# Token mixing, an MLP and a normalized MLP on one core: normalization moved to ScalarE, weight conversions begun earlier, one ring for inner features

## The chip, the cores and the metric

The kernel runs on one core of one Trainium2 chip. The metric is the device time of one execution in microseconds; three runs of the kernel before are given, and one further execution was profiled. The engines are named as the profile does: PE (TensorE, with PEld for its weight loads), DVE (VectorE), ACT (ScalarE), POOL (GpSimd) and SP (SyncE, whose queue issues nearly all DMAs).

## The reference

Attention over 4 batches, 8 heads, 576 positions and 64 columns a head, causal in a window of 128 with a slope per head; then a block that mixes tokens and channels; then a normalized MLP. Cut to what matters:

```python
attn = softmax(where(mask, scale * q @ k.T + bias, -1e9)) @ v     # B, H, S, D = 4, 8, 576, 64
x = attn.transpose(0, 2, 1, 3).reshape(B, S, H * D)               # 512 columns
h = relu(x.transpose(0, 2, 1) @ w_tok1) @ w_tok2                  # 576 -> 256 -> 576
u = x + h.transpose(0, 2, 1)
x = u + relu(u @ w_ch1) @ w_ch2                                   # 512 -> 1536 -> 512
xn = (x - mean) / sqrt(var + 1e-6) * g_ln
out = x + relu(xn @ w2_ch1) @ w2_ch2                              # 512 -> 2048 -> 512
```

The weights come as 64-bit floats and everything is held in float32.

## The kernel before

**The work.** The 4 x 576 rows are 18 tiles of 128 rows; `u` holds them in SBUF from attention to the end. A float32 product is made of three matmuls on rounded parts: each operand is split into hi (a rounded copy, mostly on ACT) and lo (the operand minus hi, on DVE or POOL), and `mm3` adds hi x hi, hi x lo and lo x hi. A float64 weight tile is converted by `load_f64`: two DMAs (`rh`, `rw`), one instruction on ACT (`e`, L414) and four on DVE (`s` twice, L417 and L419; `m`, L421; the result `y` or `w`, L429).

**Stages.** `attention()` walks the tiles, and between the softmaxes of a tile it puts one conversion and some token mixing (`tok1`, `tok1_end`, `tok2`). Then come two MLP layers. Each goes over three chunks of tiles: 0 to 7, then 16 and 17, then 8 to 15; and in a chunk over steps of two tiles of inner features. The wide chunks multiply by Strassen's scheme with seven products (`seven_products`, L987 to L989), whose left operands `prep_wide` makes from turned quadrants of `u` (`turned`: transposes on PE, L841); the narrow chunk uses `prep_small` and `two_blocks` (L438 to L440). `relu_to` splits the inner features (L918 on ACT, L920 on DVE), and `second` (L1042 to L1044) multiplies them by the second weights and adds to `u` (DVE, L1047). In the second layer `turned` first normalizes each 128x128 block (L833, on DVE): minus mean, times rstd. Both come from `tile_stats` and `chunk_stats`, which run while another chunk is multiplied.

**Weights.** `load_w` fills a ring of 6 tiles `w` with weights in the order of use; it loads a staged copy from DRAM where there is one (`w<-d`) and converts otherwise. `stage_w` converts ahead and stores (`d<-y`). In attention, at slot n (two a tile), this decides:

```python
if W_START <= n < 2 * NTILE and (n - W_START) % W_STEP == 0:
    if len(wtiles) < W_BUFS:
        load_w(len(wtiles) + 1)
    else:
        stage_w(1)
```

With `W_START` 18 and `W_STEP` 2 this is 9 slots: 6 fill the ring, 3 stage.

**What sets the order.** Nothing runs in the order of the code: `op` only records an operation with a cost per engine that may run it, and `Plan.order` then plays a list schedule: each operation has a due time that follows from the place of PE's work behind it, engines take the most urgent one that is ready, and an operation with several engines goes where it ends first. What comes out is a fixed order for each engine's queue; each engine works through its queue strictly in that order, with semaphores between them. A change in one operation's cost or place thus moves others on all queues.

**Memory.** Pools are opened and closed by `swap`. A tile of a new pool can be written only when what lay in its place is no longer used. In the kernel before, the parts of split weights (`w1`, `w2`), the inner features `h` and the small operands `s` lie in pool `mlq`, which is opened when `tok` (token weights and features), `psb` and `pst` are closed in one step: behind the last use of all of them.

## Time and profile before

| what | value |
|---|---|
| median of 3 runs | 865.22 us |
| the runs | 863.85 to 865.59 us |
| the profiled execution | 863.28 us |
| its span, first to last instruction | 861.6 us |
| granted TensorE clock, mean | 0.992 |
| busy: PE, DVE, ACT, POOL | 834.8, 654.0, 367.7, 347.6 us |
| DMA bytes moved | 163.92 MB, 190 GB/s mean |

The granted clock is the share of TensorE's full 2.4 GHz that the throttle gave. A busy share is a mean over stages with different limits; which engine ends a wait is read in the stage. In a timeline the start of an instruction counts from the start of the span, and the bracket behind it says how long the engine had stood still before and which engine and line released it. Matmuls overlap, so their pace is the distance of their starts.

### The profile page before, as it was taken

The page shows a single profiled execution, that of the slowest core. Times are in us where ns is not written, and L with a number is a line of the kernel's source. Part 1 is how long each engine was busy: PE and PEld are TensorE (multiplying, and loading weights), DVE is VectorE, ACT ScalarE, POOL GpSimd, SP SyncE. Part 2 cuts the span into 40 slices and gives each one's busy share as a digit, 9 for nine tenths or more (in the row PEclk, how much of TensorE's full clock was granted, in tenths as well). Part 3 has the DMA queues.
Part 4 walks back from the last instruction along what each step waited for, and adds up shares of the span by engine and source line. Part 5 has one row for each costly group of instructions (what it writes and reads, how often), then busy time and mean ns, then how long its engine had stood idle before and what let it go on. Part 6 is the DMA issues. An engine that isn't in the chain of part 4 may idle for free.

```text
span 861.6 us, 13160 instructions
## 1 busy us (share of the span) xinstructions
PE 834.8 (97%) x4478; PEld 688.6 (80%) x4478; DVE 654.0 (76%) x1371; ACT 367.7 (43%) x880; POOL 347.6 (40%) x362
## 2 busy tenths in 40 slices
PE   7999999898999999999997999999999999999997
PEld 6777888676888888788886888888888888888886
DVE  5787676979888889978899956879779755555554
ACT  6888765553344535233355322333354322222221
POOL 2685444555343656522245434534145712221110
PEclk9999999989999999999999999999999999999999
DMA  8588534375778799977861521897377762221112
GB/s 294 184 226 259 186 114 148 110 239 157 246 223 275 265 328 319 355 248 250 279 211 37 194 85 64 257 300 233 126 257 216 242 215 74 74 73 49 49 50 97
DMA packets 73123, 163.92 MB, mean 190 GB/s; under 512 B 8289, under 2 KB 8417, under 8 KB 73057
## 3 DMA queue, kind: packets, MB, share of 16 engines
q1 hardware_dynamic: 72576, 161.78, 56.9%
q0 software_dynamic: 480, 1.31, 0.7%
q8 instruction: 35, 0.57, 0.3%
q14 instruction: 32, 0.25, 0.1%
HBM read 130.55 MB, written 31.20 MB: 188 GB/s over the span
## 4 chain that ended last, share of the span: by engine, by line
PE 65%; DVE 8%; DMA 1%; issue 1%; ACT 0%; SPq 0%; DVEq 0%; ACTq 0%
PE acc L1044 12%; PE acc L1042 12%; PE acc L1043 12%; PE b L987 9%; PE b L989 9%; PE b L988 9%; DVE st L833 2%; DVE u L1047 1%; DVE st L372 1%; PE b L438 1%; PE b L440 1%; PE p L841 1%; PE b L439 1%; DVE hl L920 1%; DVE xl L372 1%
## 5 line engine op out<-in xcount | busy, mean ns | idle before, releaser
L1047 DVE TENSOR_TENSOR u<-acc,u 128x512 f32<-128x512 f32 x252 | 172.3, 686 | 63.5 <-PE acc L1044 60.3
L1042 PE MATMUL acc<-w2h,hh 128*128 128x512 f32 x504 | 198.6, 394 | 2.0 <-DVE u L1047 1.3
L1044 PE MATMUL acc<-w2h,hl 128*128 128x512 f32 x504 | 197.1, 391 | 2.7 <-DVE hl L920 2.6
L1043 PE MATMUL acc<-w2l,hh 128*128 128x512 f32 x504 | 196.9, 391 | 0.0
L918 ACT ACTIVATE hh<-b 128x512 fp32r<-128x512 f32 (+1 forms) x140 | 74.5, 553 | 275.3 <-PE b L989 242.2
L989 PE MATMUL b<-xh,w1l 128*128 128x512 f32 x392 | 154.0, 393 | 2.8 <-DVE w1l L372 2.8
L987 PE MATMUL b<-xh,w1h 128*128 128x512 f32 x392 | 154.3, 394 | 2.2 <-DVE hl L920 1.2
L988 PE MATMUL b<-xl,w1h 128*128 128x512 f32 x392 | 153.5, 392 | 0.0
L920 DVE SCALAR_TENSOR_TENSOR hl<-b,hh 128x512 fp32r<-128x512 f32 (+1 forms) x140 | 85.4, 630 | 59.3 <-ACT hh L918 59.1
L372 POOL TENSOR_TENSOR w1l<-w,w1h 128x512 fp32r<-128x512 f32 (+1 forms) x53 | 68.3, 1289 | 148.9 <-ACT w1h L359 148.6
L1044 PEld LDWEIGHTS acc<-w2h,hl 128*128 128x128 f32 x504 | 94.9, 188 | 23.9 <-DVE hl L920 4.0
L1042 PEld LDWEIGHTS acc<-w2h,hh 128*128 128x128 f32 x504 | 95.2, 189 | 22.9 <-DVE u L1047 3.1
L1043 PEld LDWEIGHTS acc<-w2l,hh 128*128 128x128 f32 x504 | 95.1, 189 | 18.6
L372 POOL TENSOR_TENSOR w1l<-st,w1h 128x512 fp32r<-128x512 f32 x37 | 49.8, 1346 | 113.4 <-ACT w1h L359 102.9
L987 PEld LDWEIGHTS b<-xh,w1h 128*128 128x128 f32 x392 | 74.3, 190 | 18.8 <-DVE hl L920 2.0
L989 PEld LDWEIGHTS b<-xh,w1l 128*128 128x128 f32 x392 | 74.3, 189 | 18.8 <-DVE w1l L372 3.3
L988 PEld LDWEIGHTS b<-xl,w1h 128*128 128x128 f32 x392 | 74.2, 189 | 15.3
L414 ACT ACTIVATE e<-rh 128x512 bf16<-128x512 bf16 (+2 forms) x65 | 41.3, 636 | 65.9 <-DMA rh<-wb 39.8
L641 ACT ACTIVATE pr<-t,mn 128x128 f32<-128x128 f32 x144 | 55.9, 392 | 18.5 <-DVE mn L632 18.5
L658 POOL TENSOR_SCALAR_AFFINE_SELECT pf<-pf 128x512 f32<-128x512 f32 x64 | 42.2, 659 | 34.0 <-ACT pf L359 31.5
L372 DVE TENSOR_TENSOR b<-b,p 128x512 f32<-128x512 f32 x56 | 38.9, 695 | 19.5 <-PE b L989 19.2
L372 POOL TENSOR_TENSOR w2l<-w,w2h 128x512 fp32r<-128x512 f32 x23 | 31.1, 1357 | 47.1 <-ACT w2h L359 46.9
(117 smaller groups left out, 1373.0 us busy)
## 6 DMA issues: line engine op xcount, KB each, us to landing
w<-d SPq DMA_DIRECT2D x85, 256.0 KB, 4.1
rw<-wb SPq DMA_DIRECT2D x32, 512.0 KB, 5.0
rh<-wb SPq DMA_DIRECT2D x32, 512.0 KB, 4.4
rw<-wa SPq DMA_DIRECT2D x24, 512.0 KB, 4.2
rh<-wa SPq DMA_DIRECT2D x24, 512.0 KB, 4.6
d<-y SPq DMA_DIRECT2D x29, 256.0 KB, 4.5
keys<-kT SPq DMA_DIRECT2D x18, 256.0 KB, 4.1
q<-qT SPq DMA_DIRECT2D x18, 256.0 KB, 4.5
```

What stands on the lines that cost most here:

```text
L372: pl.op({e: cost[e] for e in on}, lambda e: ENGINE[e].tensor_tensor(get(), ga(), gb(), alu), [*several(a), *several(b), *also], several(dst))
L641: op({"ACT": 580}, lambda m=m: nc.scalar.activation(out=pr.t[:, m], in_=t.t[:, m], func=AF.Exp, bias=mn.t[:, m:m + 1], scale=-1.0, accum_o ...
L658: op({"POOL": 630}, lambda a=a: nc.gpsimd.affine_select(pf.t[:, a], pf.t[:, 1], [[0, 4], [1 - 2 * a, P]], (ALU.is_ge, ALU.is_gt)[a], 0.0, ...
L918: op({"ACT": act(n, True)}, lambda: nc.scalar.activation(out=hh.t[:, c], in_=go(), func=AF.Relu), [o], [(hh, key)])
L920: mark[0] = op({"DVE": dve(n)}, lambda: nc.vector.scalar_tensor_tensor(out=hl.t[:, c], in0=go(), scalar=0.0, in1=hh.t[:, c].bitcast(F32), ...
L987: nc.tensor.matmul(g.t, wh.t[:, w], xh.t, start=start and k == 0, stop=False, skip_group_check=True)
L988: nc.tensor.matmul(g.t, wh.t[:, w], xl.t, start=False, stop=False, skip_group_check=True)
L989: nc.tensor.matmul(g.t, wl.t[:, w], xh.t, start=False, stop=stop and k == 1, skip_group_check=True)
L1042: nc.tensor.matmul(o.t, hh.t[:, c:c + P], wh.t, start=j == 0, stop=False)
L1043: nc.tensor.matmul(o.t, hh.t[:, c:c + P], wl.t, start=False, stop=False)
L1044: nc.tensor.matmul(o.t, hl.t[:, c:c + P], wh.t, start=False, stop=j == 1)
L1047: op({"DVE": dve(DM)}, lambda o=o, i=i: nc.vector.tensor_tensor(u[i].t, o.t, u[i].t, ALU.add), [o], [u[i]])
```

## The change

Four things are changed, and the planner's order follows from them.

- **Normalizing.** L833's subtract and multiply on DVE becomes one activation on ACT: Identity with `rstd` as scale and a new column `nmr` as bias. `chunk_stats` gets one more instruction on DVE, which makes `nmr` = -mean x rstd.
- **Conversions in attention.** `W_START` goes from 18 to 12: 12 slots instead of 9, 6 of them to fill the ring, 6 to stage.
- **One ring.** The token features of `tok1_end` and the inner features of the MLPs take their tiles from one ring of 6 in a new pool `hid`, which is open from start to end. The token weights `wt2h`, `wt2l` and the small operands share one pair of tiles there (`few`).
- **Pools.** `tok` is closed by itself and `mlq`, which now holds only split weights, is opened in its place; `psb` and `pst` are closed in a step of their own. `load_w(W_BUFS)` is recorded ahead of `prep_wide`. To make room, `s` in `load_f64` has one buffer instead of two, and `even` has 256 columns instead of 280.

```diff
-EVEN = 280
+EVEN = 256
-WT_SHIFT, WT_START, WT_STEP, SHIFT_AT, W_START, W_STEP = 0, 2, 1, 7, 18, 2
+WT_SHIFT, WT_START, WT_STEP, SHIFT_AT, W_START, W_STEP = 0, 2, 1, 7, 12, 2
...
-    for name in ("const", "big", "wa", "raw", "cvt", "small"):
+    for name in ("const", "big", "wa", "raw", "cvt", "small", "hid"):
...
+    nmr = buf("const", [P, NTILE], F32, "nmr")
...
-        s = buf("cvt", [P, DM], BF16, "s", 2)
+        s = buf("cvt", [P, DM], BF16, "s", 1)
...
+    def few():
+
+        return [buf("hid", [P, 2, S + P], F32R, "few" + p) for p in "hl"]
...
-    wt2h = buf("tok", [P, 2, S + P], F32R, "wt2h")
-    wt2l = buf("tok", [P, 2, S + P], F32R, "wt2l")
+    wt2h, wt2l = few()
...
+    def hidden():
+        return [buf("hid", [P, CW], F32R, "h" + p, H_BUFS) for p in "hl"]
...
-            hh = buf("tok", [P, DM], F32R, f"h1h{t}", 2)
-            hl = buf("tok", [P, DM], F32R, f"h1l{t}", 2)
+            hh, hl = hidden()
...
-                op({"DVE": 250}, lambda i=i, j=j, g=get[j]: nc.vector.tensor_scalar(
-                    x.t[:, j], g(), mv.t[:, i, 0:1], rstd.t[:, i:i + 1], ALU.subtract, ALU.mult),
-                    [u[i], (mv, i), (rstd, i)], [(x, j)])
+                op({"ACT": 330}, lambda i=i, j=j, g=get[j]: nc.scalar.activation(
+                    out=x.t[:, j], in_=g(), func=AF.Identity, bias=nmr.t[:, i:i + 1], scale=rstd.t[:, i:i + 1]),
+                    [u[i], (nmr, i), (rstd, i)], [(x, j)])
...
+        sh, sl = few()
...
-            x = [buf("mlq", [P, CW], F32R, f"s{p}{j}") for p in "hl"]
-            split_x(x, b, True)
-            out += [(x, m * HW) for m in range(2)]
+            copy((sh, j), lambda j=j: sh.t[:, j, :CW], b, lambda b=b: b.t, CW, ("ACT",), True)
+            minus((sl, j), lambda j=j: sl.t[:, j, :CW], b, lambda b=b: b.t, (sh, j),
+                  lambda j=j: sh.t[:, j, :CW].bitcast(F32), CW, ("DVE",))
+            out += [(sh, sl, j, slice(m * HW, (m + 1) * HW)) for m in range(2)]
...
+        op({"DVE": 190}, lambda: nc.vector.scalar_tensor_tensor(
+            out=nmr.t[:, c], in0=mv.t[:, c, 0], scalar=-1.0, in1=rstd.t[:, c], op0=ALU.mult, op1=ALU.mult),
+           [(mv, i) for i in tiles] + [(rstd, i) for i in tiles], [(nmr, i) for i in tiles])
...
+    load_w(W_BUFS)
+    swap(["tok"], [("mlq", {})])
+    swap(["psb", "pst"], [("psn", {"space": PSUM}), ("psc", {"space": PSUM})])
     xs, pieces = prep_wide(0, steps[0][2])
     for _ in pieces:
         pass
-    load_w(W_BUFS)
-    swap(["tok", "psb", "pst"], [("psn", {"space": PSUM}), ("psc", {"space": PSUM}), ("mlq", {})])
```

What the planner makes of it, at three places. The first is PE's queue at the seam, from the last token tile (`tok`, made of `h1h`, `wt2h`) to the first product (`b0`, made of `xh00`, `w1h`). Before:

```order
L729 MATMUL tok_2412<-h1l1_2324,wt2h_114 128x512
L730 MATMUL tok_2412<-h1h1_2318,wt2l_119 128x512
L1104 MATMUL b3_2444<-xh00_2129 128x512
L987 MATMUL b0_2462<-xh00_2129,w1h_2442 128x512 [waits Activation_49]
L988 MATMUL b0_2462<-xl00_2149,w1h_2442 128x512
L989 MATMUL b0_2462<-xh00_2129,w1l_2452 128x512 [waits DVE_49]
```

And now:

```order
L993 MATMUL b0_2416<-xh00_2152,w1h_2371 128x512 [waits Activation_49]
L994 MATMUL b0_2416<-xl00_2168,w1h_2371 128x512
L995 MATMUL b0_2416<-xh00_2152,w1l_2385 128x512 [waits Pool_49]
...
L995 MATMUL b0_2416<-xh01_2315,w1l_2385 128x512
L735 MATMUL tok_2430<-hh_2340,fewh_117 128x512 [waits DVE_49]
...
L737 MATMUL tok_2467<-hh_2349,fewl_122 128x512
L1116 MATMUL b3_2498<-xh00_2152 128x512
L993 MATMUL b0_2416<-xh40_2266,w1h_2371 128x512 [waits Activation_49]
L994 MATMUL b0_2416<-xl40_2299,w1h_2371 128x512
L995 MATMUL b0_2416<-xh40_2266,w1l_2385 128x512
L993 MATMUL b0_2416<-xh41_2473,w1h_2371 128x512 [waits Activation_49]
L994 MATMUL b0_2416<-xl41_2500,w1h_2371 128x512 [waits DVE_49]
```

The first product stood behind all token tiles and a weight-free matmul; now it stands ahead of the last three token tiles, its lo part comes from POOL, and behind the last token tile follows another product of the same weight, whose fourth operand `xl41` comes from DVE.

The second place is DVE's queue there, from the last updates of `u` to the lo part of the second weight. Before:

```order
L372 TENSOR_TENSOR st_2424<-w_1534,w_1632 128x256 [waits Pool_49]
L733 TENSOR_TENSOR u17_2227<-tok_2412,u17_2227 128x512 [waits PE_49]
L372 TENSOR_TENSOR st_2420<-st_2420,w_1534 128x256 [waits Pool_49]
L419 SCALAR_TENSOR_TENSOR s_2408<-e_2358,s_2408 128x256 [waits DVE_49]
L372 TENSOR_TENSOR st_2424<-w_1534,st_2420 128x256 [waits DVE_49]
L372 TENSOR_TENSOR w1l_2452<-w_1534,w1h_2442 128x512 [waits Activation_49]
L372 TENSOR_TENSOR w1l_2458<-st_2420,w1h_2449 128x512 [waits DMASW1_49,DMASW2_49,DMASW0_49,Activation_49]
```

And now:

```order
L374 TENSOR_TENSOR st_2480<-w_1550 128x256
L740 TENSOR_TENSOR u17_2252<-tok_2467,u17_2252 128x512 [waits PE_49]
L374 TENSOR_TENSOR st_2480<-st_2480,w_1505 128x256 [waits DVE_49]
L374 TENSOR_TENSOR xl41_2500<-p0_2461,xh41_2473 128x512
L374 TENSOR_TENSOR st_2485<-w_1505,st_2480 128x256 [waits DVE_49]
L423 TENSOR_SCALAR m_2515<-rw_2233 128x512 [waits DMAHW1_49]
L374 TENSOR_TENSOR w1l_2517<-st_2480,w1h_2502 128x512 [waits Activation_49]
```

The lo part `w1l` of the first weight has left DVE's queue here; `xl41` stands behind `u17` and one subtraction, and the second weight's lo part behind three more instructions.

The third place is the change of layer: four of the last normalizations (`st<-u`), in DVE's queue before:

```order
L1047 TENSOR_TENSOR u_1640<-acc,u_1640 128x512
L1047 TENSOR_TENSOR u_1759<-acc,u_1759 128x512
L920 SCALAR_TENSOR_TENSOR hl<-b_5378,hh 128x512
L372 TENSOR_TENSOR st<-st,p_5579 128x512
L372 TENSOR_TENSOR xl_5609<-p_5579,xh_5598 128x512
L833 TENSOR_SCALAR st<-u_760,mv,rstd 128x128
L833 TENSOR_SCALAR st<-u_889,mv,rstd 128x128
L833 TENSOR_SCALAR st<-u_1004,mv,rstd 128x128
L833 TENSOR_SCALAR st<-u_1107,mv,rstd 128x128
```

And the last four now, in ACT's queue:

```order
L840 ACTIVATE st<-u_1110,nmr,rstd 128x128
L361 ACTIVATE xh_5627<-st 128x512
L924 ACTIVATE hh<-b_2498 128x512
L924 ACTIVATE hh<-b_2301 128x512
L361 ACTIVATE w2h<-w 128x512 x2
L361 ACTIVATE xh_5660<-st 128x512
L840 ACTIVATE st<-u_324,nmr,rstd 128x128
L840 ACTIVATE st<-u_445,nmr,rstd 128x128
L840 ACTIVATE st<-u_547,nmr,rstd 128x128
L840 ACTIVATE st<-u_669,nmr,rstd 128x128
```

The normalizations stood behind updates of `u`, an inner feature's lo part and operands; now they stand behind an operand's copy, two relus (`hh`), two copies of second weights (`w2h`) and one more operand.

## Rows read from the trace of the kernel before

**Rows 1.** The page, part 1: busy us, share of the span, instructions.

```profile
PE 834.8 (97%) x4478; PEld 688.6 (80%) x4478; DVE 654.0 (76%) x1371; ACT 367.7 (43%) x880; POOL 347.6 (40%) x362
```

**Rows 2.** Stretches: length, busy (instructions) per engine, clock, DMA share, GB/s.

```profile
100.00:120.00 20.00, 20.00 (x190) 16.50 (x187) 13.68 (x65) 14.32 (x48) 10.27 (x14) 1.00 0.47 154
160.00:180.00 20.00, 16.57 (x64) 12.91 (x63) 19.55 (x27) 9.79 (x17) 12.05 (x10) 0.83 0.41 126
200.00:220.00 20.00, 16.97 (x76) 13.40 (x75) 19.77 (x30) 7.83 (x15) 11.53 (x10) 1.00 0.69 217
460.00:480.00 20.00, 15.50 (x64) 12.01 (x62) 19.34 (x33) 8.15 (x14) 15.23 (x14) 0.91 0.19 50
```

**Rows 3.** Timeline, PE, seam: start, us, instruction, [idle before, releaser].

```profile
169.89 0.50 PE L987 MATMUL b<-xh,w1h 128*128 128x512 f32 x1 [0.61 <-ACT w1h L359]
...
173.45 0.80 PE L989 MATMUL b<-xh,w1l 128*128 128x512 f32 x1 [2.82 <-DVE w1l L372]
174.04 0.63 PE L987 MATMUL b<-xh,w1h 128*128 128x512 f32 x1
...
178.73 0.60 PE L989 MATMUL b<-xh,w1l 128*128 128x512 f32 x1
...
182.59 0.39 PE L988 MATMUL b<-xl,w1h 128*128 128x512 f32 x1
182.82 0.40 PE L989 MATMUL b<-xh,w1l 128*128 128x512 f32 x1
```

**Rows 4.** Timeline, DVE, the seam.

```profile
170.10 0.68 DVE L733 TENSOR_TENSOR u<-tok,u 128x512 f32<-128x512 f32 x1
170.70 0.89 DVE L372 TENSOR_TENSOR st<-st,w 128x256 f32<-128x256 f32 x1
...
172.72 0.68 DVE L372 TENSOR_TENSOR w1l<-w,w1h 128x512 fp32r<-128x512 f32 x1
```

**Rows 5.** Timeline, PE, second step of the first MLP layer.

```profile
210.34 0.49 PE L987 MATMUL b<-xh,w1h 128*128 128x512 f32 x1 [1.23 <-DVE hl L920]
...
214.95 0.50 PE L1044 MATMUL acc<-w2h,hl 128*128 128x512 f32 x1 [1.80 <-DVE hl L920]
```

**Rows 6.** Waits: us in total, times, longest.

```profile
PE p L841 <- DVE st L833: 5.4, 4, 3.1
```

**Rows 7.** Timeline, PE, the change of layer.

```profile
465.61 1.25 PE L841 MATMUL p<-ident,st 128*128 128x128 f32 x4 [3.08 <-DVE st L833]
466.51 0.78 PE L1042 MATMUL acc<-w2h,hh 128*128 128x512 f32 x1
...
469.22 0.44 PE L1042 MATMUL acc<-w2h,hh 128*128 128x512 f32 x1
```

**Rows 8.** Timeline, DVE, the change of layer.

```profile
453.30 1.88 DVE L833 TENSOR_SCALAR st<-u,mv,rstd 128x128 f32<-128x128 f32 x7
...
458.09 4.06 DVE L833 TENSOR_SCALAR st<-u,mv,rstd 128x128 f32<-128x128 f32 x4
```

**Rows 9.** Timeline, POOL, the change of layer.

```profile
459.57 2.50 POOL L372 TENSOR_TENSOR w2l<-w,w2h 128x512 fp32r<-128x512 f32 x2
```

**Rows 10.** Groups by line and shape: count, busy us, mean ns, idle before.

```profile
L641 ACT ACTIVATE pr<-t,mn 128x128 f32<-128x128 f32 x144 | 55.9, 392 | 18.5 <-DVE mn L632 18.5
...
L421 DVE TENSOR_SCALAR m<-rw 128x512 uint32<-128x512 uint32 x56 | 35.2, 628 | 0.3
L359 ACT ACTIVATE w1h<-w 128x512 fp32r<-128x512 f32 x56 | 34.9, 624 | 4.4 <-PE b L988 2.5 <-issue 1.8
...
L429 DVE SCALAR_TENSOR_TENSOR y<-m,s 128x512 f32<-128x512 uint32 x35 | 31.1, 889 | 0.9 <-POOL w L474 0.7
...
L419 DVE SCALAR_TENSOR_TENSOR s<-e,s 128x256 int32<-128x256 int32 x56 | 28.2, 504 | 0.3
...
L417 DVE TENSOR_SCALAR s<-e 128x256 int32<-128x256 int32 x56 | 24.3, 433 | 0.4 <-ACT e L414 0.4
...
L359 ACT ACTIVATE w1h<-w 128x256 fp32r<-128x256 f32 x28 | 11.7, 417 | 0.1
```

More of the change, by code (lines that the diff above doesn't have):

```diff
@@ L908, in w_split @@
         return hi, lo
-    def hidden():
-        return [buf("mlq", [P, CW], F32R, "h" + p, H_BUFS) for p in "hl"]
     mark = [0]
@@ L1161, in block_kernel @@
         pl.emit()
-    for n in ("mlq", "mlr", "mlp", "even", "psc", "psn", "psm", "small", "cvt", "raw", "wa", "big", "const", "dram"):
+    for n in ("mlq", "mlr", "mlp", "even", "psc", "psn", "psm", "hid", "small", "cvt", "raw", "wa", "big", "const", "dram"):
         pl.pools[n].release()
```

4 lines of the change are left out of this document (2 added, 2 removed).

## The prediction

> **What bounds the kernel now.** I read the page first: TensorE is busy for 834.8 of 861.6 us, 97% of the span [rows 1], and no other engine is above 80%. The change takes no matmul away, so it can only win time in which TensorE stands still or runs slowly. The table by stretches says where that is. Between 100 and 120 us, in attention, TensorE is busy for all 20.00 us at a granted clock of 1.00, while DVE has 6.3 us free and ACT 5.7. In three stretches DVE is full instead (19.55, 19.77 and 19.34 of 20) and TensorE is not (16.57, 16.97 and 15.50) [rows 2]. These three places are what the change aims at; the timelines tell what each costs.
>
> The seam from token mixing to the first MLP. TensorE has the last token matmul done and waits 0.61 us for the hi part of the first weight and 2.82 us for its lo part, which DVE makes [rows 3]. DVE is late since it serves its queue in order: the last update of u, a subtraction of 0.89, and only at 172.72 that lo part [rows 4]. After this pause the matmuls start 0.43 us apart (12 starts from 174.04 to 178.73) instead of 0.23 [rows 3]; the granted clock of this stretch averages 0.83 [rows 2], that is, part of it ran at the lower level, 1.2 of 2.4 GHz, after TensorE had idled twice. From 173.45 to 178.73 twelve matmuls took 5.28 us where 12 x 0.23 = 2.76 would do: 2.5 lost. The seam costs 0.61 + 2.82 + 2.5 = 5.9 us.
>
> The second step of the first layer. Two waits for the lo part of an inner feature, 1.23 and 1.80 us, both on DVE [rows 5]: 3.0 us, at full clock.
>
> The change of layer. TensorE's transposes wait for normalized tiles from DVE: 5.4 us in four waits, the longest 3.1 [rows 6]. Then six matmuls from 466.51 to 469.22 take 2.71 us where 6 x 0.23 = 1.38 would do [rows 7], with 0.91 as granted clock of that stretch [rows 2]: 1.3 lost. Together 6.7 us. The cause can be read: seven normalizations took 1.88 us (0.27 each), and four a moment later took 4.06 (1.0 each) [rows 8], while POOL subtracted from 459.57 to 462.07 [rows 9]. DVE's work from SBUF to SBUF is held up by POOL's.
>
> All three together are 5.9 + 3.0 + 6.7 = 15.6 us. That is the most that the change can bring.
>
> **The change part by part.**
>
> The first weights next to the ring. In the new order TensorE does the first product before the last three token tiles, and its lo part is made by POOL ahead of them. Both waits of the seam go. What is late next is the product behind the last token tile: its fourth left operand, xl41, is made by DVE after u17 and a subtraction. By the rows of before that is 0.68 + 0.89 + 0.68 (as a lo part of 512 columns) = 2.25, and TensorE has 5 matmuls of 0.23 = 1.15 to do meanwhile [rows 3, 4]. That leaves 1.1; with the way from TensorE to DVE and back, which no row shows apart, I take 1.4 us, and I expect no half clock after it, since waits of 1.23 and 1.80 in the second step left the clock at 1.00 [rows 2, 5]. Term: -5.9 + 1.4 = **-4.5** (bounds -5.9, and 0 if a wait as long as the old one returns with its slow clock).
>
> Conversions earlier. Three more tiles are converted in attention and staged, and in exchange three fewer are converted straight into the ring later. Counted in the order, DVE does one conversion instead of four in the second step and four instead of three in the third. The second step's waits of 3.0 mostly go; I leave 0.7 for the third step: **-2.3** (bounds -3.0 and 0). In attention each conversion takes DVE 0.43 + 0.50 + 0.63 + 0.89 = 2.45 us, and ACT about what a copy of 512 columns takes, 0.62 [rows 10], so three take 9.2 us of both. The cover is the 6.3 us that DVE and the 5.7 that ACT have free in each 20 us there, at a TensorE of 20.00 [rows 2]. Without cover the whole 9.2 would show. I take **+0.5** (bounds 0 and +9.2), near the row of attention, where conversions already run and TensorE never stops. On SP's queue the raw loads move ahead of a few loads of q, keys and v; those are asked for three tiles ahead, which covers it.
>
> Normalizing on ScalarE. 72 instructions leave DVE and go to ACT. ACT has no row with two pointer operands on 128 columns. From below: one pointer costs 0.392 us [rows 10]. From above: twice the 256-column copy, 0.83. Between: 256 columns more cost 0.624 - 0.417 = 0.207 us, so 128 columns without a pointer are about 0.313, one pointer adds 0.079, and two give 0.47, the value I take, as it is nearest to the row of the same width. That is 72 x 0.47 = 33.8 us on ACT over the kernel, against 8.15 busy of 20 at the change of layer [rows 2]. DVE's queue loses just the instructions that were held up there. What is late next is ACT: ahead of the last four normalizations stand two copies of x, two relus and two splits of w2, 6 x 0.62 = 3.7, and the four themselves are 1.9, while TensorE has twelve matmuls, 2.8 us, to do. At worst 2.8 us of wait, at best none if ACT is ahead; I take 1.5. Term: -6.7 + 1.5 = **-5.2** (bounds -6.7, and the rival below). The small new instruction per chunk for -mean x rstd runs on DVE while another chunk's products run, at no cost; without that cover it delays one chunk by less than a 256-column instruction, 0.42, three times.
>
> Shared ring, one buffer fewer for s, a smaller memset. The token features take the ring first, three batches deep; the first MLP step uses the places after them: no wait. s is written, used and written again by DVE alone, in order, so one buffer adds no wait to DVE; ACT's next e can start later by one conversion, under the cover above. Four more DMAs of 256 KB net (three stagings and their loads, fewer copies of used weights): 217 GB/s at a share of 0.69 is 314 GB/s [rows 2], 0.8 us each, 3.3 us if nothing covered them; the queues have a third free, so 0.
>
> Everything is ordered anew by the planner, and outside the three places TensorE hardly waits, so a new order can only lose there: **+1.0** (bounds 0 and +3.1, the largest wait of before [rows 6]).
>
> Sum: -4.5 - 2.3 + 0.5 - 5.2 + 1.0 = **-10.5 us**. The profiled execution took 863.28 us, so its counterpart takes 852.8; the median of the runs shown is 865.22, 1.9 above the profiled one, so I predict **854.7 us**.
>
> **The rivals.**
>
> The seam stays (0.20). DVE is full there [rows 2], and the products after the first still need three subtractions and a lo part behind u17. If a pause of the old length returns, with the slow clock, the first term is 0: 865.2 - 10.5 + 4.5 = 859.2. Against it: the first product is already out of the way.
>
> All waits go (0.12): 865.2 - 15.6 = 849.6. For it: DVE has less to do in all three places.
>
> Slower: ACT becomes the late engine (0.08). ACT works in order, and eight normalizations stand ahead of a relu at the change of layer. Without the layer term the sum is -5.3. So if over a sixth of the 33.8 us lands on TensorE's path, the kernel is slower; at a third, 11.3, it takes 865.2 - 5.3 + 11.3 = 871.2. Against it: ACT is idle for 60% of that stretch, and its work is not held up by POOL as DVE's is [rows 2, 8]. The Trainium skill (ScalarE: Activation LUTs, Rules for kernel authors) speaks for this rival: it tells to add and multiply on VectorE, not ScalarE. By the undisturbed rows it is right, 0.27 against 0.47; by the disturbed ones, 1.0 each, it is not, and those are the ones that TensorE waits for [rows 8]. By that page's figures for an ACTIVATE (186 ns, 0.833 per column, 93 per pointer) one instruction is an estimated 479 ns.
>
> The conversions don't hide (0.08). The change then moves a cost instead of covering it: 9.2 in place of 0.5 gives 863.4, at the edge of no change.
>
> **How the numbers follow.** The forecast itself has 0.52, and 851 to 858 as its own range. The range is 849.5 to 861.5: it takes in the case in which everything goes and the one in which the seam stays, and leaves out the last two rivals and tails, about 0.2. A difference under 0.2%, 1.7 us, cannot be told from none. Faster: 0.52 + 0.20 + 0.12 + 0.04 of the last rival = 0.88; same 0.05; slower 0.07.
>
> **What would show it.** In the profile of the changed kernel TensorE should wait about 1.4 us near the seam, for xl41 from DVE, at a granted clock of about 1.00 instead of 0.83; in the second step the waits for hl should be under 1 us in sum; at the change of layer the transposes should wait for ACT, not DVE, under 3 us in all, at a clock near 1.00. DVE's busy time should fall by some 35 us and ACT's rise by some 30. The prediction is wrong if TensorE waits in attention, if the clock still falls at either place, or if relus of the second layer come late.

## The result, and the profile after

| what | before | changed |
|---|---|---|
| median, on one chip | 864.76 us (863.85 to 865.59, 5 runs) | 855.04 us (852.57 to 856.19, 5 runs) |
| ratio of the times | 1 | 0.9883 (95%: 0.9864 to 0.9902) |
| the profiled execution | 863.28 us | 856.19 us |
| its span | 861.6 us | 854.5 us |

The change saves 9.7 us by the medians, where 854.7 us was forecast: the time is right. Where it came from is partly another matter. Both kernels issue the same 4478 matmuls, so the start of the k-th one can be set beside the start of the k-th one of before; every entry below is the difference of two such distances. The stretches left out differ by less than 0.1. The entries sum up to -7.8; from the last matmul to the end of the span the changed kernel takes 0.7 us more, and -7.1 is what the two spans differ by.

| stretch, by number of the matmul | before, us | after less before | forecast |
|---|---|---|---|
| 150 to 1200, attention | 24.0 to 144.0 | +0.5 | +0.5 |
| 1200 to 1450, the seam | 144.0 to 199.0 | +1.2 | -4.5 |
| 1450 to 1600, the second step | 199.0 to 236.2 | -2.8 | -2.3 |
| 1600 to 2600 | 236.2 to 447.8 | -0.6 | } +1.0 |
| 2600 to 2760, the change of layer | 447.8 to 488.8 | -4.0 | -5.2 |
| 3000 to 3150 | 543.2 to 577.2 | +1.1 | } |
| 3150 to 3750, the second layer's narrow chunk | 577.2 to 691.5 | -3.2 | none |

Two things bear on how the entries are read. Each comes from one profiled execution. And the k-th matmul is not the same one everywhere: in the changed kernel the seam holds four transposes of 128 columns where the kernel before has four matmuls of 512 columns, which the changed kernel does in the second step. At the pace of the rows that is about 0.5 us, so for the same work the seam is nearer to +1.7 and the second step to -3.3. The same holds for every kernel with the changed kernel's pools; conv12_old, late_pool and the kernels named norm_act, below, have the places of before.

The page of the changed kernel, part 1, and its table by stretches, as [rows 1] and [rows 2] of before:

```profile
PE 830.8 (97%) x4478; PEld 685.8 (80%) x4478; DVE 638.1 (75%) x1311; ACT 394.3 (46%) x952; POOL 338.5 (40%) x353
```

```profile
100.00:120.00 20.00, 20.00 (x168) 16.11 (x164) 14.99 (x53) 15.32 (x49) 11.69 (x16) 1.00 0.50 153
160.00:180.00 20.00, 16.16 (x73) 12.39 (x73) 19.76 (x28) 11.60 (x22) 13.62 (x12) 1.00 0.43 131
180.00:200.00 20.00, 17.91 (x78) 14.62 (x79) 13.51 (x24) 7.30 (x13) 5.11 (x6) 0.91 0.83 283
200.00:220.00 20.00, 19.94 (x88) 16.20 (x87) 17.17 (x27) 7.00 (x13) 8.02 (x7) 1.00 0.52 160
460.00:480.00 20.00, 17.87 (x79) 14.15 (x79) 18.63 (x33) 10.05 (x20) 13.62 (x14) 1.00 0.26 81
```

Attention still keeps TensorE at 20.00, and the second step is full (19.94 against 16.97). The seam is not: TensorE has 16.16 and then 17.91, and the half clock, which stood in 160 to 180 (0.83), now stands in 180 to 200 (0.91). TensorE's timeline there, as [rows 3]:

```profile
172.11 0.39 PE L993 MATMUL b<-xh,w1h 128*128 128x512 f32 x1
174.34 0.50 PE L994 MATMUL b<-xl,w1h 128*128 128x512 f32 x1 [1.84 <-DVE xl L374]
...
178.34 0.40 PE L995 MATMUL b<-xh,w1l 128*128 128x512 f32 x1
182.09 0.50 PE L993 MATMUL b<-xh,w1h 128*128 128x512 f32 x1 [3.36 <-DVE hl L926]
...
183.00 0.63 PE L993 MATMUL b<-xh,w1h 128*128 128x512 f32 x1
...
185.56 0.63 PE L993 MATMUL b<-xh,w1h 128*128 128x512 f32 x1
```

The first wait is the forecast one, for xl41: 1.84 us, and the matmuls behind it start 0.23 apart. The second was not in the forecast: the next product needs a bank whose inner feature DVE has not read out, 3.36 us, and then the pace is 0.43, that of the lower clock level; this half clock costs 1.9 us. DVE's and POOL's timelines say why:

```profile
175.42 0.68 DVE L374 TENSOR_TENSOR w1l<-st,w1h 128x512 fp32r<-128x512 f32 x1
176.02 1.77 DVE L431 SCALAR_TENSOR_TENSOR y<-m,s 128x512 f32<-128x512 uint32 x1
177.72 0.96 DVE L374 TENSOR_TENSOR w1l<-w,w1h 128x256 fp32r<-128x256 f32 x1
178.60 0.81 DVE L419 TENSOR_SCALAR s<-e 128x256 int32<-128x256 int32 x1
179.33 1.77 DVE L374 TENSOR_TENSOR w1l<-w,w1h 128x512 fp32r<-128x512 f32 x1
181.02 0.41 DVE L421 SCALAR_TENSOR_TENSOR s<-e,s 128x256 int32<-128x256 int32 x1
181.36 0.68 DVE L926 SCALAR_TENSOR_TENSOR hl<-b,hh 128x512 fp32r<-128x512 f32 x1
```

```profile
177.20 1.19 POOL L374 TENSOR_TENSOR st<-st,w 128x256 f32<-128x256 f32 x1
178.47 0.79 POOL L374 TENSOR_TENSOR st<-w,st 128x256 f32<-128x256 f32 x1
179.29 1.26 POOL L374 TENSOR_TENSOR w1l<-st,w1h 128x512 fp32r<-128x512 f32 x1
```

hl's input lies ready since 176.7 (ACT's relu). Ahead of it stand five instructions that take 0.68, 0.41, 0.28, 0.68 and 0.41 where POOL is idle, 2.5 us, and 5.7 here, beside POOL's subtractions.

At the change of layer no transpose waits for a normalized tile any more; one wait of more than 0.3 us is left, for an update of u on DVE. The line of the normalizations gives their price on ACT (shortest, median and longest, in ns). The longest is hardly above the shortest, though 16 of the 72 lie almost wholly beside a subtraction of POOL's:

```profile
467.48 0.50 PE L1048 MATMUL acc<-w2h,hh 128*128 128x512 f32 x1 [1.91 <-DVE u L1053]
```

```profile
L840 ACT ACTIVATE st<-u,nmr,rstd x72: 479/483/496, 391.1 to 664.6; 128x128 f32<-128x128 f32 x72
```

### The profile page after: what moved, and what is told of

It is laid out like the page before. It is cut to its first block, busy times and chain, and to the rows that moved or that the text cites. A ratio compares the mean times of both kernels' runs of the same rounds, so it can differ in the third digit from the quotient of the medians.

```text
span 854.5 us, 13205 instructions
## 1 busy us (share of the span) xinstructions
PE 830.8 (97%) x4478; PEld 685.8 (80%) x4478; DVE 638.1 (75%) x1311; ACT 394.3 (46%) x952; POOL 338.5 (40%) x353
## 4 chain that ended last, share of the span: by engine, by line
PE 83%; DVE 7%; ACT 4%; DMA 2%; issue 2%; POOL 1%; SPq 1%; ACTq 0%; DVEq 0%; POOLq 0%
PE acc L1048 12%; PE acc L1050 12%; PE acc L1049 12%; PE b L993 9%; PE b L995 9%; PE b L994 9%; PE ps_v L608 3%; PE ps_s L596 3%; PE p L848 1%; PE b L442 1%; PE b L441 1%; PE b L440 1%; PE ps_t L653 1%; DVE st L374 1%; PE tok L735 1%
```

## The experiments

The first question was which part of the change gives what; the second, what holds the seam. Two kinds of kernel were run: some keep the order of all queues as it is and move or re-assign single operations, the others let the planner order anew. Each was timed beside the kernel before on the same chip, whose median lay between 863.6 and 864.1 us (864.76 for the changed kernel). The table sums up all of them, with the stretches of the ledger above (less before, us); the two runs marked * have another pace of matmuls, which covers the stretches.

| run | median, us | ratio (95%) | seam | second step | change of layer | narrow chunk |
|---|---|---|---|---|---|---|
| changed kernel | 855.04 | 0.9883 (0.9864 to 0.9902) | +1.2 | -2.8 | -4.0 | -3.2 |
| norm_act_old_order * | 871.94 | 1.0096 (1.0080 to 1.0112) | | | | |
| norm_act_old_even | 861.53 | 0.9968 (0.9953 to 0.9983) | +0.1 | +1.6 | -0.6 | -1.7 |
| norm_act_replanned | 858.42 | 0.9941 (0.9928 to 0.9953) | +0.2 | 0.0 | -4.0 | -3.1 |
| norm_dve_new_order | 863.38 | 0.9988 (0.9974 to 1.0001) | -0.5 | -2.8 | -0.7 | +1.9 |
| conv12_old | 860.02 | 0.9953 (0.9936 to 0.9969) | +0.6 | -3.6 | 0.0 | -0.1 |
| conv18_new | 853.79 | 0.9884 (0.9867 to 0.9901) | +1.0 | -2.0 | -4.0 | -3.2 |
| late_pool | 855.52 | 0.9903 (0.9889 to 0.9917) | +1.8 | -3.6 | -4.0 | -2.1 |
| even248 * | 863.90 | 1.0001 (0.9988 to 1.0014) | | | | |
| seam_pool | 852.50 | 0.9866 (0.9848 to 0.9885) | -2.5 | -2.9 | -4.1 | -3.2 |
| seam_order | 852.26 | 0.9865 (0.9847 to 0.9882) | -2.6 | -2.8 | -2.5 | -3.2 |
| best_order | 857.60 | 0.9929 (0.9914 to 0.9943) | +2.6 | -2.9 | -2.4 | -3.2 |
| best_order2 | 851.43 | 0.9852 (0.9839 to 0.9864) | -2.0 | -2.9 | -5.2 | -2.2 |

The half clock moves these entries by nearly 2 us without any change of order. Up to the change of layer norm_dve_new_order has the queues of the changed kernel, and at the seam the same waits (1.83 and 3.37 us), but its profiled execution kept the clock at 1.00 there, and its entry is -0.5 instead of +1.2:

```profile
180.00:200.00 20.00, 16.63 (x80) 13.43 (x79) 15.09 (x25) 7.92 (x14) 6.60 (x8) 1.00 0.86 285
```

### Normalizing alone, and a surprise

**norm_act_old_order.** The kernel before, its order untouched, with L833 emitted as the activation of the diff (and `nmr` made behind `rstd` in the same operation):

```diff
+    nmr = buf("const", [P, NTILE], F32, "nmr")
...
-                op({"DVE": 250}, lambda i=i, j=j, g=get[j]: nc.vector.tensor_scalar(
-                    x.t[:, j], g(), mv.t[:, i, 0:1], rstd.t[:, i:i + 1], ALU.subtract, ALU.mult),
+                op({"DVE": 250}, lambda i=i, j=j, g=get[j]: nc.scalar.activation(
+                    out=x.t[:, j], in_=g(), func=AF.Identity, bias=nmr.t[:, i:i + 1], scale=rstd.t[:, i:i + 1]),
```

> The kernel before in its own order of all queues; only the 72 normalizations are emitted on ACT instead of DVE, each at the place in time where it stood, and one small instruction behind rstd makes the new column. Theory A (the normalizations on DVE were what TensorE waited for, since POOL held them up): the waits of the transposes for st, 5.4 us, and most of the 1.3 us of slow clock go, ACT takes about 0.48 us for each; 6 us less, at most 6.7, so about 859 us. Theory B (the gain at the change of layer comes from the new order, not from the engine): DVE's next late work, an update of u, takes the wait over, as it does in the changed kernel (1.9 us there), or ACT's own queue is late; less than 3 us gained, 862 to 866 us.

Measured: 871.94 us, 8 slower than before. Neither theory had that. No wait explains it: between 700 and 830 us, where TensorE never stops in either kernel, its matmuls start 0.2315 us apart on the mean of 562, against 0.2267 of 574 before. Two of before, and four of norm_act_old_order, at a granted clock of 1.00:

```profile
749.75 0.39 PE L987 MATMUL b<-xh,w1h 128*128 128x512 f32 x1
749.97 0.39 PE L988 MATMUL b<-xl,w1h 128*128 128x512 f32 x1
```

```profile
749.61 0.39 PE L990 MATMUL b<-xh,w1l 128*128 128x512 f32 x1
749.84 0.40 PE L988 MATMUL b<-xh,w1h 128*128 128x512 f32 x1
750.08 0.40 PE L989 MATMUL b<-xl,w1h 128*128 128x512 f32 x1
750.32 0.39 PE L990 MATMUL b<-xh,w1l 128*128 128x512 f32 x1
```

What differs from before in that stretch is where the tiles lie: 18 more columns (96 bytes with the padding) push up all tiles that are laid from the low end of SBUF.

**norm_act_old_even** and **even248** tested this, each by one number (`even` is a tile at the high end that nothing reads; its size shifts the tiles laid below it):

```diff
 norm_act_old_even, against norm_act_old_order
-EVEN = 280
+EVEN = 256
 even248, against the changed kernel
-EVEN = 256
+EVEN = 248
```

> The run norm_act_old_order once more (the kernel before in its own order, normalizations on ACT), but with EVEN at 256 as in the changed kernel. Theory D: what made that run 8 us slower than before is no wait but the pace of the matmuls of the MLPs, 0.2315 us from start to start instead of 0.2267, in all of its 2688 matmuls of 512 columns (2688 x 0.0048 = 12.9 us); and this pace depends on where the tiles lie in SBUF: the new column nmr moves all tiles that are laid from the low end by 96 bytes, so that weights and inner features start at 32 above a multiple of 64 bytes, and the operands xh and xl, laid from the high end, at a multiple of 64. EVEN at 256 moves those by 96 bytes too. Then the pace is 0.2267 again and the time is 872 - 13 = 859 us, the 859 expected of normalizing on ACT alone. Theory E (the pace comes from ACT's work or from something else in that run): it stays at 0.2315 and the time at 870 to 873 us.

> The changed kernel with one size changed: EVEN 248 instead of 256, which moves the tiles laid from the high end (xh, xl and st among them) by 32 bytes, to multiples of 64, while weights and inner features stay at 32 above. The order of all queues is the same. Theory D: the matmuls' pace in the MLPs falls to about 0.2315 us, 13 us in all, 867 to 869 us. Theory E: 855 us as before, pace 0.2267.

Measured, with the start addresses that each program gives its tiles (bytes beyond a multiple of 64):

| kernel | split weights, hh, hl | xh, xl | pace, us | time, us |
|---|---|---|---|---|
| before | 0 | 0 | 0.2267 | 863.9 |
| norm_act_old_order | 32 | 0 | 0.2315 | 871.94 |
| norm_act_old_even | 32 | 32 | 0.2267 | 861.53 |
| changed kernel | 32 | 32 | 0.2267 | 855.04 |
| even248 | 32 | 0 | 0.2311 | 863.90 |

Theory D holds in both directions: with the two groups of operands 32 bytes out of step the MLPs' matmuls are 2% slower, 8.9 and 10.4 us. (Expected were 12.9; the mean was taken over all of them, and it varies by kind.) So `EVEN` is no mere memset: with it at 280 xh and xl of the changed kernel would start at 0 modulo 64, as in even248, and the new column `nmr` would have cost about what the whole change brings. Why the addresses matter is not shown. It is not simply that a matmul is slow when its own two operands are out of step: in norm_act_old_order, between 700 and 830 us, the first products (xh or xl with w1) start 0.234 us apart and the second ones (w2 with hh or hl) 0.2295, and the operands of the second ones all start at 32. The reverse case, 0 for the weights and 32 for xh and xl, was not tried.

With the pace out of the way, normalizing on ACT in the old order brings 2.3 us, not 6 (its entry of +1.6 for the second step is half clock in the profiled execution, 0.91 between 200 and 220 us). At the change of layer TensorE then waits for ACT, as the third rival had it. Its timeline, and ACT's ahead of it, in norm_act_old_even:

```profile
463.95 0.86 PE L842 MATMUL p<-ident,st 128*128 128x128 f32 x2 [2.31 <-ACT st L834]
```

```profile
461.16 1.14 ACT L360 ACTIVATE w2h<-w 128x512 fp32r<-128x512 f32 x2
462.40 0.60 ACT L360 ACTIVATE xh<-p 128x512 fp32r<-128x512 f32 x1
462.90 0.62 ACT L360 ACTIVATE xh<-st 128x512 fp32r<-128x512 f32 x1
463.42 0.87 ACT L834 ACTIVATE st<-u,nmr,rstd 128x128 f32<-128x128 f32 x2
```

**norm_act_replanned** is the same with the planner told, so that it can lay ACT's queue for it:

```diff
-                op({"DVE": 250}, lambda i=i, j=j, g=get[j]: nc.scalar.activation(
+                op({"ACT": 330}, lambda i=i, j=j, g=get[j]: nc.scalar.activation(
...
-                    [u[i], (mv, i), (rstd, i)], [(x, j)])
+                    [u[i], (nmr, i), (rstd, i)], [(x, j)])
```

> The kernel before with normalizations on ACT and EVEN at 256, as in norm_act_old_even, but now the planner is told of it (cost on ACT instead of DVE) and orders all queues anew. Pools, ring and conversions stay those of before. Theory A (normalizing on ACT is worth the waits at the change of layer once the queues are laid for it): 4.2 us there and 1.8 at about 655 us go, the seam and the second step stay: 857 to 859 us. Theory B (in the old order it gave 2.3 us, and most of the changed kernel's gain needs the other parts): 861 to 863 us.

Measured: 858.42 us. Theory A: -4.0 at the change of layer and -3.1 in the narrow chunk, the two stretches of the changed kernel to a tenth, while the seam and the second step stay as they were:

```profile
160.00:180.00 20.00, 16.58 (x65) 12.85 (x64) 19.53 (x27) 9.23 (x17) 12.56 (x11) 0.83 0.46 145
...
200.00:220.00 20.00, 16.99 (x76) 13.40 (x75) 19.55 (x31) 7.55 (x14) 10.21 (x9) 1.00 0.73 241
460.00:480.00 20.00, 17.86 (x79) 13.89 (x78) 18.64 (x33) 10.32 (x20) 14.26 (x14) 1.00 0.23 74
```

**norm_dve_new_order**, the counterpart: the changed kernel in its own order, with the normalizations emitted on DVE.

```diff
-                op({"ACT": 330}, lambda i=i, j=j, g=get[j]: nc.scalar.activation(
-                    out=x.t[:, j], in_=g(), func=AF.Identity, bias=nmr.t[:, i:i + 1], scale=rstd.t[:, i:i + 1]),
+                op({"ACT": 330}, lambda i=i, j=j, g=get[j]: nc.vector.tensor_scalar(
+                    x.t[:, j], g(), mv.t[:, i, 0:1], rstd.t[:, i:i + 1], ALU.subtract, ALU.mult),
```

> The changed kernel in its own order of all queues; only the 72 normalizations are emitted on DVE again. Theory A (the engine decides): transposes wait for st from DVE again, at the change of layer and about 190 us later, 4 to 8 us in sum, so 859 to 863 us. Theory B (the new order decides): these waits stay under 2 us in sum and the time is within 2 us of the changed kernel's 855.

Measured: 863.38 us, the upper end of theory A; the two stretches lose their gain (-0.7 and +1.9). But the waits for st are 2.7 us in sum, less than the 4 to 8 expected; the rest is for other work of DVE's that is late, and the longest near there, at 445 us, is 1.74 us for an addition. In DVE's queue two of the normalizations take 1.98 us beside POOL, as in [rows 8]:

```profile
464.76 0.59 DVE L840 TENSOR_SCALAR st<-u,mv,rstd 128x128 f32<-128x128 f32 x2
...
465.88 1.98 DVE L840 TENSOR_SCALAR st<-u,mv,rstd 128x128 f32<-128x128 f32 x2
```

### The second step: conversions, ring or pool

**conv12_old** is the kernel before with one number changed, **conv18_new** the changed kernel with that number put back, **late_pool** the changed kernel with the pools opened as before:

```diff
 conv12_old (and, the other way round, conv18_new)
-WT_SHIFT, WT_START, WT_STEP, SHIFT_AT, W_START, W_STEP = 0, 2, 1, 7, 18, 2
+WT_SHIFT, WT_START, WT_STEP, SHIFT_AT, W_START, W_STEP = 0, 2, 1, 7, 12, 2
 late_pool
-    load_w(W_BUFS)
-    swap(["tok"], [("mlq", {})])
-    swap(["psb", "pst"], [("psn", {"space": PSUM}), ("psc", {"space": PSUM})])
     xs, pieces = prep_wide(0, steps[0][2])
     for _ in pieces:
         pass
+    load_w(W_BUFS)
+    swap(["tok", "psb", "pst"], [("psn", {"space": PSUM}), ("psc", {"space": PSUM}), ("mlq", {})])
```

> The changed kernel with W_START back at 18: 9 conversions in attention instead of 12, ordered anew by the planner, all else as in the changed kernel. If the earlier conversions took the second step's waits away (as the forecast says), these come back, 3.0 us and more between 200 and 230 us, with a little gained in attention: 857 to 859 us. If the ring and the pools did it, the second step stays without waits and the time is 854 to 856 us.

> The changed kernel with one part undone: mlq is opened together with psn and psc, behind the last use of tok, psb and pst, and the last weight is loaded and the first operands are made in the order of before; ring, few, conversions and normalizations stay as in the changed kernel. The planner orders anew. Theory F (the early pool is what lets the first weights' parts be made ahead, and with them the second step's waits go): two or more us of waits return between 200 and 230 us and the first product stands behind the token tiles again: 857 to 860 us. Theory G (the place of the pool decides nothing, the seam costs its 7 to 9 us either way, as it does before and after the change): 853 to 856 us.

> The kernel before with one number changed, W_START 12 instead of 18: three more tiles are converted in attention and staged; pools, rings, s and the engine of the normalizations stay those of before. The second step's waits (3.4 us over the pace) went in late_pool (12, new ring, old place of the pool) and nearly so in conv18_new (18, new ring, new place), and stayed in norm_act_replanned (18, old ring, old place). Theory H (the earlier conversions are enough by themselves, as the forecast says, and the new ring and pool are a second way to the same end): under 1 us of waits from 200 to 230 us, 860 to 862 us. Theory I (the ring, or the single buffer of s, which both of those runs have, is what removed them): 3 us of waits stay there, 863 to 866 us.

Measured: conv18_new 853.79, late_pool 855.52 (theory G), conv12_old 860.02 us (theory H). The earlier conversions alone take the second step's waits away, as the forecast had it; here TensorE is full from 200 to 220:

```profile
200.00:220.00 20.00, 20.00 (x92) 16.57 (x91) 19.02 (x32) 8.07 (x15) 8.75 (x7) 1.00 0.80 258
```

But conv18_new does without them and is as fast as the changed kernel (a little below both ranges expected, by the way of the second): what is new in its pools and rings takes most of the same waits away a second time.

```profile
200.00:220.00 20.00, 19.58 (x86) 15.86 (x86) 17.06 (x31) 6.99 (x13) 8.80 (x9) 1.00 0.73 226
```

There DVE still does four conversions in these 20 us, but they take 8.6 us of DVE instead of the 11.8 of before, with less of POOL beside them. The two gains are one gain and do not add. What the earlier conversions win in the second step of the changed kernel (0.8 us against conv18_new) it gives back elsewhere: 0.4 in attention, and 2.2 between 236 and 448 us, where it waits 1.32 us for an update of u and conv18_new does not. What in the planner's order makes that difference is not shown, and neither is which of ring, `s` and early pool does it in conv18_new. And the early pool, which puts the first product ahead of three token tiles, saves nothing by itself: late_pool is as fast as the changed kernel (the intervals overlap), and its seam, +1.8 with the places of before, is that of the changed kernel counted for the same work, +1.7. Each was taken with half clock.

### The seam

**seam_pool** and **seam_order** leave the changed kernel's order as it is but for a few operations. In seam_pool three subtractions go from POOL to DVE, behind hl; in seam_order hl goes ahead of w1l, and the conversion's y and s, s behind both:

```diff
 seam_pool, in Plan.emit
-        for k in self.order():
+        line = self.order()
+        for k, j in ((1106, 1092), (1110, 1106)):
+            line.remove(k)
+            line.insert(line.index(j) + 1, k)
+        for k in (1106, 1110, 1108):
+            self.taken[k] = 'DVE'
...
+        for k in line:
...
 seam_order, in Plan.emit
-        for k in self.order():
+        line = self.order()
+        for k, j in ((901, 1104), (951, 901), (952, 951)):
+            line.remove(k)
+            line.insert(line.index(j) + 1, k)
+        for k, j in ((1092, 1104),):
+            line.remove(k)
+            line.insert(line.index(j), k)
...
+        for k in line:
...
```

The numbers are the planner's: 1092 is hl, 1104 the w1l of 512 columns, 901 y, 951 and 952 the two instructions of s, 1106, 1110 and 1108 the second step's two sums st and its w1l.

> The changed kernel in its own order, but for three subtractions of the second step's first weights that POOL ran at 177 to 181 us, beside DVE's work at the seam: they go to DVE, behind the lo part hl for which TensorE waited 3.36 us. Theory A (POOL's work holds up DVE's, instructions of 0.68 and 0.41 us took 1.77 and 0.96): with POOL idle in that stretch DVE's five instructions ahead of hl take about 2.5 us instead of 6.3, hl is made 3 us earlier, the wait falls under 0.7 us and the half clock behind it (1.9 us) goes; about 851 us, 4 to 5 less. Theory B (DVE has too many instructions ahead of hl, whatever POOL does): the wait stays above 2.5 us, 854 to 856 us.

> The changed kernel in its own order, but for DVE's queue at the seam: hl moves ahead of the lo part w1l of 512 columns, and three instructions of a conversion (y and twice s) that stood ahead of them move behind. POOL's work stays. Theory A and theory B both let the wait fall: two instructions instead of six stand ahead of hl; by the held-up durations (0.96 for the one of 256 columns) hl is done near 178, w1l near 179.8, and TensorE waits under 1.3 us at the place where it waited 3.36, with the clock at 1.00: 851 to 852 us. Theory C (DVE is simply full at the seam, so a wait removed comes back at the next operand): a wait of 2 us or more for another product of DVE's within the next 15 us, and 854 to 856 us.

Measured: 852.50 and 852.26 us, 2.5 and 2.8 us below the changed kernel by the medians (the intervals of the ratios overlap), and in both the wait of 3.36 is gone. In seam_pool the same five instructions, in the same order, with POOL idle after 175.40:

```profile
174.18 1.77 DVE L440 SCALAR_TENSOR_TENSOR y<-m,s 128x512 f32<-128x512 uint32 x1
175.87 0.41 DVE L383 TENSOR_TENSOR w1l<-w,w1h 128x256 fp32r<-128x256 f32 x1
176.20 0.28 DVE L428 TENSOR_SCALAR s<-e 128x256 int32<-128x256 int32 x1
176.40 0.68 DVE L383 TENSOR_TENSOR w1l<-w,w1h 128x512 fp32r<-128x512 f32 x1
177.01 0.41 DVE L430 SCALAR_TENSOR_TENSOR s<-e,s 128x256 int32<-128x256 int32 x1
177.34 0.68 DVE L935 SCALAR_TENSOR_TENSOR hl<-b,hh 128x512 fp32r<-128x512 f32 x1
```

w1l takes 0.68 instead of 1.77, the others 0.41 and 0.28 instead of 0.96 and 0.81, and DVE even has three instructions more to do. For the durations that is theory A, and against B.

That the wait went altogether is not the edits' work alone. In both runs the wait for xl41 stays (1.83 and 1.84), and now the half clock follows that one; it costs 1.4 and 1.6 us, and by that TensorE needs hl later. even248, with the changed kernel's order, shows this without any edit of the seam: there too the half clock follows the wait for xl41 (1.84), POOL's third subtraction comes later (178.23, behind the w1l of 512 columns, which takes 0.68), and the wait for hl is 1.11 instead of 3.36. Counted from the matmul with xl41, TensorE at full clock needs hl after 4.2 us; hl is done after 7.7 in the changed kernel (174.34 to 182.04), after 5.5 in seam_pool (172.48 to 178.02) and after 3.8 in seam_order (172.89 to 176.66). So at full clock an estimated 1.3 us of wait would be left in seam_pool, and none for hl in seam_order; there, as best_order2 below shows, the next addition to b is late in its place.

**best_order** and **best_order2** were tries at a faster kernel, with more such moves: updates of u (2258, 2260, 1630, 2515) ahead of what stood before them, m (839, and 949, the load that follows it) behind the last token tile's hl (998), and in best_order a new order of DVE's whole seam. The moves of best_order2:

```diff
...
+        for k, j in ((901, 1104), (951, 901), (952, 951), (839, 998), (949, 839)):
+            line.remove(k)
+            line.insert(line.index(j) + 1, k)
+        for k, j in ((1092, 1104), (2258, 2205), (2260, 2214), (1630, 1729), (2515, 2575)):
+            line.remove(k)
+            line.insert(line.index(j), k)
...
```

> The changed kernel, with DVE's queue put in another order at five places where TensorE waits: at the seam xl41 and the sum st for the first weight ahead of u17, conversions behind hl; the three updates of u for which TensorE waited 1.32, 1.91 and 0.81 us ahead of subtractions or of m, and m behind the first hl of the last token tile. Nothing else moves but what hangs on these. Theory A (each of these waits is a matter of DVE's order and of POOL beside it): of the waits of 1.20, 1.84, 3.36, 1.32, 1.91 and 0.81 us and of 1.9 us at half clock about 9 go: 845 to 847 us. Theory C (DVE is full at the seam, the waits only change their name): the seam keeps 3 us or more, 849 to 851 us.

> Seam as in seam_order (hl ahead of w1l of 512 columns, three instructions of a conversion behind them); besides, m behind the first hl of the last token tile (wait of 1.20), u16 ahead of a subtraction (1.32), u4 ahead of m (0.81), and at the change of layer both u10 and u11 ahead of the subtractions of weights (1.91). In best_order xl41 did not come ahead of u17 as its text says but behind three more instructions, and b's addition came behind the conversion; both are left out here. Theory A: 3 us as in seam_order, and of the other four waits 0.8, 0.9, 0.6 and 1 us go, as best_order's profile showed for the first three: 848 to 850 us. Theory C (a wait removed comes back at the next of DVE's products): 851 to 853 us, as seam_order alone.

best_order took 857.60 us, slower than the changed kernel and outside the ranges of both theories. Its edit did not do all that its text says, as the text of best_order2 tells: xl41 came later instead of earlier, and the waits at the seam were 2.75 us for xl41 and 3.17 for the addition behind the moved conversion, each followed by half clock. best_order2 took 851.43 us, the fastest of all, 0.9852 of before; its interval overlaps those of seam_order and seam_pool. The time lies in the range of theory C, though both theories have a part: the change of layer gained 1.2 us more, while at the seam three waits stand for DVE's products again, at full clock (1.00 from 160 to 200 us). This is theory C for the seam: set against norm_dve_new_order, the changed kernel's order at full clock (-0.5), best_order2's seam (-2.0) is 1.5 us shorter, and 0.9 of these lie ahead of the first product, where moving m took a wait of 1.20 away. The three waits:

```profile
171.23 0.50 PE L1004 MATMUL b<-xl,w1h 128*128 128x512 f32 x1 [1.17 <-DVE xl L384]
...
174.06 0.50 PE L1005 MATMUL b<-xh,w1l 128*128 128x512 f32 x1 [1.20 <-DVE w1l L384]
...
180.18 0.50 PE L1003 MATMUL b<-xh,w1h 128*128 128x512 f32 x1 [2.18 <-DVE b L384]
```

## Why the prediction was right, and where it was not

**The seam (-4.5 forecast, +1.2 measured, -0.5 in the same order without half clock): wrong with either.** The first half came as written: w1l made by POOL ahead of the token tiles, a wait of 1.84 us for xl41 where 1.4 was taken, the clock at 1.00 behind it. That last part was luck: behind the same wait the clock fell in even248, seam_pool and seam_order. The step that failed is the sentence "What is late next is the product behind the last token tile": the forecast followed DVE's queue to that product and no further. Behind it the same queue, as full as before (19.76 of 20), held hl back until TensorE stood for 3.36 us and ran 1.9 us longer at half clock. Without the half clock the wait is the same (3.37 in norm_dve_new_order), and the seam still misses the term by 4 us. The price fails with the path: the five instructions ahead of hl take 2.5 us by their undisturbed rows and took 5.7 beside POOL, which the forecast had read at the change of layer and not looked for here. It is the first rival, to which 0.20 was given, and the wait came at another place than it named; the clock that falls again at the seam is one of the signs of being wrong that the forecast had set itself.

**The second step (-2.3 forecast, -2.8 measured): right**, in cause too by conv12_old (-3.6). But the forecast put the ring and the pools at nothing, and by conv18_new they do most of it without the conversions; in the changed kernel the earlier conversions save nothing on top of that (855.04 us with them, 853.79 without).

**Attention (+0.5): right.** With three conversions more, TensorE waits 0.82 us at 61.7 us for a tile `ut` of ACT's, where it waited 0.60, and 0.30 us at 78.5 for another, where it did not wait. By the forecast's own sign that is a cover that does not hold everywhere, but the price is the one given.

**The change of layer (-5.2 forecast): right in mechanism, split in two places.** ACT's instruction costs 0.483 us where 0.47 was worked out. Of the four waits in [rows 6] one, 0.89 us, does not belong to the change of layer but lies at 659 us, where the second layer's narrow chunk runs. That stretch gained 3.2 us: this wait, one of 0.55 for hl beside it, and some 1.5 that no single gap shows. With it the normalizations are worth 7.2 us in the ledger, 5.7 by the medians of norm_act_replanned. That wait in the kernel before:

```profile
659.49 0.33 PE L841 MATMUL p<-ident,st 128*128 128x128 f32 x1 [0.89 <-DVE st L833]
```

The wait that is left at the change of layer comes from DVE (1.91 for u), not from ACT (1.5): the forecast took ACT's queue as the late one, and the planner had laid it early enough. Left in the old order ACT was indeed late (norm_act_old_even), so the third rival's mechanism exists here; it is the order that avoids it. The Trainium skill's rule (ScalarE: Activation LUTs, Rules for kernel authors) to add and multiply on VectorE is right by single price, 0.483 against a median of 0.339 us on DVE, and wrong for this place: norm_dve_new_order is 8 us slower than the changed kernel.

**The rest (+1.0): about right**, +1.1 at 540 us (a wait of 0.81 for u behind a conversion) and -0.6 between 236 and 448.

**What cost nothing.** Ring, `s` and pool cost nothing, as forecast. `EVEN` was passed over as "a smaller memset"; it was what kept 9 us from being lost.

**The sum.** The terms gave -10.5; the profiled pair shows -7.1 and the medians -9.7. Against the terms the seam is 5.7 off (6.2 for the same work, and then the second step gives 1.0 back) and the change of layer 1.2; the narrow chunk gives 3.2 of it back. That the sum comes out so near is luck in part: the narrow chunk's gain, which no term had, covers half of what the seam missed. That the medians come out nearer than the profiles is chance too: the profiled execution of before lies 1.5 below its median, that of the changed kernel is the slowest of five. The forecast of DVE's busy time was wrong: it fell by 15.9 us, not 35, since nine subtractions went from POOL to DVE (362 instructions of POOL, now 353) and DVE's conversions got slower beside POOL. The second instruction of `s`, which took 504 ns on the mean [rows 10], takes 610 now:

```profile
L421 DVE SCALAR_TENSOR_TENSOR s<-e,s 128x256 int32<-128x256 int32 x56 | 34.2, 610 | 0.3
```

## What to carry to other kernels

When a change removes the wait that ends last at a place where an engine is full, follow that engine's queue through the whole stretch, not to the next consumer only, and price each instruction as it runs there, beside its neighbour, not at its undisturbed length. A part that moves between engines is worth what the order of the queues makes of it: here the same 72 instructions were worth 2.3 us in the old order and 5.7 in one laid for them. And compare the pace of the main engine's instructions between two kernels before explaining a difference by waits: a column of 72 bytes more can shift every operand. Since the half clock came and went between executions of one order, a stretch that holds it is not priced by a single profile: here the same seam was +1.2 in one and -0.5 in another.

## What the runs showed of the hardware that was not expected

- Start addresses: with split weights and inner features at 32 (modulo 64 bytes) and xh and xl at 0, float32 matmuls of 512 columns start 0.2311 to 0.2315 us apart on the mean; with all of them at 0, or all at 32, 0.2267. The matmuls of the second weights, whose own operands agree, are slower too.
- POOL holds up only some of DVE's work. In the changed kernel's MLPs, `u<-acc,u`, with one operand in PSUM, took 0.63 to 0.69 us in all 252 cases, 71 of them for at least four fifths beside a subtraction of POOL's; `y<-m,s`, with both in SBUF, took 0.68 alone and up to 1.77 beside one; `m<-rw`, with one in SBUF, 0.42 alone and up to 1.54. The Trainium skill (SBUF — State Buffer, SBUF: two separate sides) has a port pair that DVE and GpSimd share as an exclusive lock, taken by DVE's operations with two SBUF inputs or in a 2-port mode; these numbers agree for the operands in SBUF, and 1.77 is 0.68 and most of POOL's own 1.26 to 1.30. That `m<-rw` runs in such a mode no run here shows.
- The half clock is not certain to follow a wait. At the seam, in the same order, the wait of 3.36 us was followed by it in the changed kernel and that of 3.37 in norm_dve_new_order was not; the wait of 1.84 for xl41 was not followed by it in the changed kernel and was in even248. At the change of layer the wait of 1.91 us left the clock at 1.00 in the changed kernel, and one of 1.93 us in the same order was followed by half clock in seam_order:

```profile
460.00:480.00 20.00, 18.07 (x73) 14.37 (x72) 17.86 (x36) 8.19 (x15) 12.07 (x12) 0.91 0.41 142
```

- The first 40 us, the same work in these three kernels, are granted different clocks from one execution to the next: 0.94 between 20 and 40 us in the changed kernel's profile, 1.00 in seam_pool's, 0.87 in norm_dve_new_order's. Matmul 150, counted from 0, starts at 24.11, 22.28 and 26.15 us. Up to 3.9 us of a difference between two profiles lie there, so stages are compared by distances behind it.

```profile
20.00:40.00 20.00, 19.65 (x184) 15.21 (x183) 14.64 (x69) 15.67 (x54) 13.02 (x19) 0.94 0.68 195
```

```profile
20.00:40.00 20.00, 19.65 (x190) 15.14 (x188) 15.14 (x70) 17.20 (x63) 14.28 (x21) 1.00 0.69 211
```

```profile
20.00:40.00 20.00, 19.73 (x169) 15.23 (x170) 14.14 (x57) 15.14 (x56) 11.79 (x19) 0.87 0.55 164
```
